# A two-branch attention kernel: operation order from a refitted plan, the middle score tiles in one exponential, value products after all scores

## The chip, the cores and the metric

The kernel runs on one core of a Trainium2 chip. Five engines work side by side, each through its own queue in order: TensorE (PE, matmuls; its weight loads are listed apart as PEld), VectorE (DVE), ScalarE (ACT), GpSimd (POOL) and SyncE (SP), which here only issues transfers. They wait for each other by semaphores. The metric is the device time from the first to the last instruction, in microseconds.

## The reference, cut to what matters

Two attention branches read the same x (2048 tokens, 640 columns, 32 heads of 20), and a gate mixes them.

```python
# branch A: linear attention with softmax feature maps
phi(t) = concat(softmax(t @ w_phi), softmax(-t @ w_phi))
kv, z  = sum_s phi(k) v,  sum_s phi(k)
a      = (phi(q) @ kv) / (phi(q) @ z + 1e-6) @ wo
# branch B: 4 segments of 512 tokens, one after the other
p      = softmax(q k^T * 20**-0.5 + causal mask)          # inside the segment
mem    = (phi(q) @ M) / (phi(q) @ z + 1e-6)               # phi(t) = t+1 if t>0 else exp(t)
o      = sigmoid(beta) * mem + (1 - sigmoid(beta)) * p @ v
M, z   = M + phi(k)^T v, z + sum phi(k)                   # carried to the next segment
b      = o @ wo
out    = g * a + (1 - g) * b,   g = sigmoid(sum(x * gate_w))
```

## The kernel before, in words

**A plan made when the program is built.** The class `Graph` holds a list of operations. Each call of `op` adds one with the engines it may run on, a duration that the plan believes, the tiles it reads and writes, and a priority `pr` (lower goes first). `schedule` then plays the machine forward: for every engine it looks at the ready operations, computes with `est` when each could start (engine free, operands ready, buffers and PSUM banks free), and takes the one with the lowest priority among those that could start within `DELTA` = 0.12 of the earliest. The result is a fixed order for each queue. `emit` writes the instructions in this order with the semaphore waits that the data needs. The believed durations are therefore no part of the program that runs. They only decide the order, and with it which wait stands ahead of which work.

**Priorities.** They are sums of constants: branch B's step g of segment n has 8n + g, its projections, value projection, memory and output work have offsets such as `BN`, `VN`, `MM`, `OT`; branch A's key work starts at `AK` and steps by 1.021 for each of its 16 token tiles, its query work at `AQ` and steps by 4.075 for each of four segments. So the two branches are woven together over the whole span.

**Branch B, one step (`b_step`, L909).** One of 8 head groups (4 heads) of one of 4 segments; 32 steps. Scores are made transposed, key tile by key tile (128 keys each, j = 0 to 3), for 4 heads at once, in three bursts (L923): j = 0 (4 matmuls of 512 columns); j = 1 and 3 together (384 and 128 columns in one bank of each head); j = 2 (256 columns). Each burst fills four PSUM banks. For the first two bursts these are two separately claimed pairs of banks; for the third, one claim of two neighbouring pairs (`joint`, tile size 5 in `tile_avail`). ScalarE turns the scores into exponentials in SBUF (`expT`): two ACTIVATEs of 128x1024 for each of the first two bursts (`expair`, L933), one of 128x1024 over all four banks for the third (`exp2`, L952). GpSimd zeroes what the causal mask hides (L938, four selects of 128x512 in a step). The value products `pv` (L978, 40 matmuls of 21 columns) come in two halves: b = 0 for query tiles 0 and 1, which need key tiles 0 and 1; b = 1 for query tiles 2 and 3, which need all. They wait for the step's last burst in the order (`after=[self.lastqk]`). From segment 1 on, the memory products (L982) go with them. `combine` on VectorE (L1002 to L1027) divides, scales and adds the two into `oB`. Two buffers of `expT` alternate.

**Branch B, the rest.** `b_proj` (L782, L803) projects queries, keys and values of a segment; `b_mem` updates the memory (L858, L872); `b_out` transposes `oB` by a transfer (in the last segment by TensorE, L1046).

**Branch A.** `a_k`, once per token tile: key and value projections (L1065, L1066), two exponentials (L1072), sum, reciprocal and product on VectorE (L1080, L1082, L1083), a transposing transfer of the result (`TT`, issued at L614), and then two adds of the transposed tile into `acc` (L1090, L1092). `a_kv` (L1113, L1124) makes the products with the values, four tiles at a time. `a_q` (L1167 to L1237) does the query side of one segment, `final` (L1268, L1269) both output projections of a token tile into one sum.

The lines that the plan's view of the machine rests on, and the claim for the last wait:

```python
def d_act(n):
    return 0.16 + n * 0.00079
...
    self.dma("sp", ..., transpose=True, dur=1.36, lat=2.5, name="TT")
...
    self.op("pe", ..., pv, ..., claim=[self.oB], after=[self.lastqk], name=f"PV{n},{g}")
```

Of the kernel before, what the change touches and what calls it, by code (L numbers as in the profile page):

```python
# [7 lines left out]
ALU = mybir.AluOpType  # L8
AX = mybir.AxisListType

# [21 lines left out]
def d_act(n):  # L32
    return 0.16 + n * 0.00079


def d_dve(n, mode=1, psum=False):
    return (0.15 if psum else 0.08) + n / (960.0 * mode)
# [6 lines left out]
def d_mm(*ns):  # L44
    return sum(max(n / 2200.0, 0.035) for n in ns)


class Op:
    __slots__ = ("name", "engs", "dur", "fn", "reads", "writes", "claim", "pr", "deps", "users", "tiles", "nleft", "stream",
                 "start", "end", "idx", "dma", "inc", "key", "val", "vc", "lat", "extra", "succ")  # L50


class Tile:
    def __init__(self, name, shape, dtype, pool):
        self.name, self.shape, self.dtype, self.pool = name, shape, dtype, pool
        self.ops = []
        self.h = {}
        self.qk = False
        self.slot = None
        self.prev = ()  # L60
        self.t = None
        self.left = 0

# [38 lines left out]
class Graph:  # L102
# [5 lines left out]

    def op(self, engs, dur, fn, R=(), W=(), pr=0.0, claim=(), name="", dma=False, lat=0.0, after=()):
        o = Op()  # L110
        if isinstance(engs, str):
            engs = (engs,)
        if not isinstance(dur, dict):
            dur = {e: dur for e in engs}
        o.engs, o.dur, o.fn, o.pr, o.name, o.dma, o.lat = engs, dur, fn, pr, name, dma, lat
        o.claim = list(claim)
        deps = list(after)
        tl = []
        for (t, k) in R:
            deps += t.touch(o, k, False)  # L120
            tl.append(t)
        for (t, k) in W:
            deps += t.touch(o, k, True)
            tl.append(t)
        o.reads, o.writes = R, W
        o.tiles = list(dict.fromkeys(tl))
        o.deps = [d for d in dict.fromkeys(deps) if d is not o]
        o.idx = len(self.ops)
        o.stream = None
        o.succ = []  # L130
        o.inc = False
        o.extra = []
        self.ops.append(o)
        return o

    def schedule(self):
# [39 lines left out]
        def tile_avail(t, commit=False):  # L176
# [5 lines left out]
            if isinstance(p, PsumPool):  # L182
                n = t.shape
                if n == 1:
                    best = None
                    for b in range(8):
                        if bank_occ[b] is None:
                            lone = bank_occ[b ^ 1] is None
                            c = (bank_t[b] + (0.3 if lone else 0.0), b)
                            if best is None or c < best:  # L190
                                best = c
                    if best is None:
                        return None
                    if not self.filler_ok(fillers, t):
                        return None
                    if commit:
                        claim_banks(t, [best[1]])
                    return bank_t[best[1]]
# [18 lines left out]
            for s in p.slots:  # L217
                m = 0.0
                ok = True
                for oc in s.occ:  # L220
                    if oc.left > 0:
                        ok = False
                        break
                    for d in oc.ops:
                        m = max(m, d.end)
                if ok and (best is None or m < best[0]):
                    best = (m, s)
# [19 lines left out]

        def est(o, e):
            st = max(free[e], dep_time(o, e))
            qs = [t for t in o.tiles if t.qk and t.slot is None]  # L250
            if qs:
                ps = sorted(max(bank_t[2 * k], bank_t[2 * k + 1]) for k in range(4) if bank_occ[2 * k] is None and bank_occ[2 * k + 1] is None)
                if len(ps) < len(qs):
                    return None
                st = max(st, ps[len(qs) - 1] + LAT)
            for t in o.claim:
                a = tile_avail(t)
                if a is None:
                    return None
                st = max(st, a + LAT)  # L260
# [17 lines left out]
        while done < n:  # L278
# [39 lines left out]
            free[e] = o.end  # L318
            if o.dma:
# [46 lines left out]
    def emit(self):  # L366
# [6 lines left out]
        for q in qs:  # L373
            for i in range(RING):
                allsem[("q", q, i)] = qsem[q][i]
        for o in self.order:
            ds = dict.fromkeys(o.deps)
            for t in o.tiles:
                if any(w[0] is t for w in o.writes):
                    for d in t.prev:  # L380
                        ds[d] = None
            o.extra = [d for d in ds if d is not o]
# [70 lines left out]
class GatedMix(Graph):  # L453
# [174 lines left out]
    def setup(self):  # L628
# [41 lines left out]
        def sel(v, pat, base, cm):  # L670
            op("pool", 0.6, lambda e: e.affine_select(v(), v(), pattern=pat, compare_op=ALU.is_ge, fill=0.0, base=base,
                                                      channel_multiplier=cm), W=[(Mm, "*")], pr=-4)
# [16 lines left out]
        for c in range(NCH):  # L689
# [6 lines left out]
            op("pe", 0.3, tr, R=[(xr, "*"), (idt, "*")], W=[(pt, 0)], pr=-30 + 0.1 * c, name="x0tr")  # L696
# [33 lines left out]
    def fuse(self, wT, Wd, ic, pr):  # L730
# [12 lines left out]
        self.op("pe", 6 * 0.06, mm, R=[(wT, "*"), (BD, "*")], W=[(pt, 0), (pt, 1)], pr=pr, name="fuse")  # L743
# [16 lines left out]
    def b_proj(self, n):  # L760
# [3 lines left out]
        if n == 0:  # L764
            pts = [self.pst("q0", 1) for c in range(NCH)]
            for kc in range(NCH):
# [5 lines left out]
                self.op("pe", 1.3, mm, R=[(self.WB, (0, a, kc)) for a in range(2)] + [(xT, (0, kc))], W=[(p, 0) for p in pts], pr=base - 3 + 0.1 * kc, name="q0proj")  # L772
# [19 lines left out]
        for i in range(4):  # L792
            self.dma("sp", qk[32 * i:32 * i + DH, 5:8, :, :].rearrange("p c w t -> p c (w t)"), scr.rearrange("(m i d) w t -> i d m (w t)", i=4, m=3)[i],
                     R=[(sT, "*")], W=[(qk, f"r{i}")], pr=prr, dur=0.36, lat=2.6, name="relr")
        for tl in range(4):
# [11 lines left out]
            self.op("act", 0.22, lambda e, t=t, pt=pt: e.activation(self.eg[:, t:t + 1], self.pf(pt, 1, 128, 1), ACT.Exp, scale=-1.0),  # L807
# [22 lines left out]
    def b_mem(self, n):  # L830
# [6 lines left out]
        for c in range(NCH):  # L837
            self.dma("sp", lambda c=c: pk[:, :, 128 * c:128 * (c + 1)], qk[:, c, 1, :], R=[(qk, (1, c))],
                     W=[(pk, c)], pr=8 * n + self.KT[0] + self.KT[1] * c, transpose=True, dur=(1.27 if n else 1.7), lat=2.0, name="kT")
        for tl in range(4):  # L840
# [7 lines left out]
            self.op("dve", 0.56, lambda e, tl=tl, tm=tm: e.tensor_tensor(pk[:, tl, :], pk[:, tl, :], tm[:, :], ALU.min),  # L848
# [12 lines left out]
        self.op("pe", 40 * 0.04, mm, R=[(pk, ("t", tl)) for tl in range(4)] + [(vt, tl) for tl in range(4)] + [(vt, "one")], W=[(mp, 0), (mp, 1)], pr=pr, name="Mmm")  # L861
# [14 lines left out]
    def b_pq(self, n):  # L876
        qk = self.qk[n % 2]
        self.pq = {}
        for c in range(NCH):
# [7 lines left out]
            self.op("dve", 0.47, lambda e, pq=pq, tm=tm: e.tensor_tensor(pq[:, :], pq[:, :], tm[:, :], ALU.min),  # L887
# [14 lines left out]
    def b_step(self, n, g):  # L902
# [7 lines left out]
        def burst(js, joint=False):  # L910
            if joint:
                pt = self.pst("QK", 5)
# [14 lines left out]
            self.lastqk = self.op("pe", 0.14 + sum((LSEG - 128 * j) / 2370.0 + 0.03 for j, _ in js), mm, R=rqk, W=pts, claim=[ex], pr=s, name=f"QK{n},{g}")  # L927
# [12 lines left out]
        p0 = burst([(0, 0)])  # L940
        expair(p0, 0, 0)
        mask(0, lambda: ex[:, :, 0:128], [[0, 4], [1, 128]], 512, [(0, 0), (0, 1)])
        p1 = burst([(1, 0), (3, 384)])
        expair(p1, 512, 1)
        mask(1, lambda: ex[:, :, 512:640], [[0, 4], [1, 128]], 512, [(1, 0), (1, 1)])
        mask(3, lambda: ex[:, :, 896:1024], [[0, 4], [1, 128]], 512, [(1, 0), (1, 1)])
        p2 = burst([(2, 0)], True)[0][0]
# [5 lines left out]
        self.op("act", d_act(1024), exp2, W=[(p2, i) for i in range(4)] + [(ex, 2)], pr=s + 0.02, name="exp2")  # L953
# [4 lines left out]
        for b in range(2):  # L958
# [26 lines left out]
            self.op("pe", cnt * 0.0285 + (0.06 * len(parts) if am else 0), pv, R=R, W=[(ad, b if n else 0)], pr=s + self.PVP[0], claim=[self.oB], after=[self.lastqk], name=f"PV{n},{g}")  # L985
# [46 lines left out]
    def b_out(self, n):  # L1032
        oB = self.oB
        for qi in range(4):
# [4 lines left out]
            if n < SEG - 1:  # L1039
                self.dma("sp", lambda oT=oT: oT[:, :, :], lambda qi=qi: oB[:, qi, :], R=rd, W=[(oT, "*")], pr=pr, transpose=True, dur=1.28, lat=2.2, name="oTB")  # L1040
# [7 lines left out]
            self.op("pe", 5 * 0.055, tr, R=rd + [(self.ident, "*")], W=[(pt, 0)], claim=[oT], pr=pr, name="oTBtr")  # L1048
# [3 lines left out]
    def a_k(self, t):  # L1052
# [27 lines left out]
        self.op("dve", 1.42, lambda e: e.tensor_reduce(rz[:, :], Ev(), axis=AX.X, op=ALU.add),  # L1080
                R=[(E, 0), (E, 1)], W=[(rz, "*")], pr=pr, name="Zsum")
        self.op("dve", 0.5, lambda e: e.reciprocal(rz[:, :], rz[:, :]), W=[(rz, "*")], pr=pr, name="Zrec")  # L1082
        self.op("dve", d_dve(1280), lambda e: e.tensor_tensor(  # L1083
            Ev(), Ev(), rz[:, :].rearrange("p (h o) -> p h o", o=1).to_broadcast([128, 2 * H, DH]), ALU.mult),
            R=[(rz, "*")], W=[(E, 0), (E, 1)], pr=pr, name="Anorm")
        self.spread(E, T2, pr)
# [10 lines left out]
    def spread(self, E, T, pr):  # L1097
        self.dma("sp", lambda: T[:, :, :], lambda: E[:, :, :].rearrange("p s n -> p (s n)"), R=[(E, 0), (E, 1)], W=[(T, 0), (T, 1)], pr=pr, transpose=True,
                 dur=1.36, lat=2.5, name="TT")
        return T  # L1100

    def a_kv(self, S):
        pr = self.AK[0] + self.AK[1] * (4 * S + 4)
        ts = [4 * S + i for i in range(4)]
        for s in range(2):
# [10 lines left out]
            self.op("pe", 20 * 0.08, mm, R=[(self.Et[t], s) for t in ts] + [(self.vt[t], "*") for t in ts], W=[(pt, 0), (pt, 1)], pr=pr, name="kv")  # L1116
# [10 lines left out]
    def a_fin(self):  # L1127
        pr = self.AK[0] + self.AK[1] * 16
        zf, K1 = self.zf, self.KVZ1
        self.op("dve", 1.3, lambda e: e.tensor_reduce(zf[:, :, :].rearrange("p s c -> p (s c)"), self.acc[:, :, :], axis=AX.X, op=ALU.add),  # L1130
# [25 lines left out]
    def a_q(self, S):  # L1156
# [34 lines left out]
        op("pe", 1.1, zmm, R=[(ET, s) for ET in ETs for s in range(2)] + [(Mk, c) for c in range(NCH)], W=[(zt, 0)],  # L1191
# [13 lines left out]
        op("pe", 0.25, rtr, R=[(rh, 0), (rh, 1), (self.ident, "*")], W=[(tp, 0)], pr=prz, name="rtr")  # L1205
        self.evac(512, lambda: rT[:, :], lambda: self.psbf[0:64, 1024 * tp.t[0]:1024 * tp.t[0] + 512], W=[(tp, 0), (rT, "*")], pr=prz, name="rT_ev", mode=2)
        for c in range(NCH):
            pt = self.pst("rb", 1)
            op("pe", 0.28, lambda e, c=c, pt=pt: e.matmul(self.pf(pt, 0, 0, LSEG), lhsT=self.Bsel[:, c, :], rhs=rT[:, :], start=True, stop=True),
# [4 lines left out]
        for tl in range(4):  # L1214
# [17 lines left out]
            op("pe", 12 * 0.062, mm, R=kall + [(ET, s) for ET in ETs for s in range(2)], W=[(pt, 0), (pt, 1)], claim=[oA, sm], pr=pru, name="U")  # L1232
# [9 lines left out]
            if S < SEG - 1:  # L1242
                self.dma("sp", lambda oT=oT: oT[:, :, :], lambda oA=oA: oA[:, :], R=[(oA, 0), (oA, 1)], W=[(oT, "*")], pr=pru + 0.5,
                         transpose=True, dur=1.28, lat=2.2, name="oTA")
            else:
# [6 lines left out]
                op("pe", 5 * 0.055, tr, R=[(oA, 0), (oA, 1), (self.ident, "*")], W=[(pt, 0)], claim=[oT], pr=pru + 0.5, name="oTAtr")  # L1252
# [102 lines left out]
```

## Time and profile before

| | before |
|---|---|
| median of 3 runs, us | 345.99 (343.73 to 347.31) |
| profiled span, us | 345.6 |
| mean granted TensorE clock | 0.965 |
| exponentials of branch B, 128x1024 (L933) | 128, 123.2 us |
| the same over four banks (L952) | 32, 32.8 us |
| masks on GpSimd (L938) | 128, 88.4 us |
| value products (L978) | 1280, 42.9 us |
| TT transfers, issue to landing | median 3.7 us |

How to read the profile: TensorE's matmuls overlap, and their ends are modelled, so a mean duration (387 ns for 512 columns) is more than the distance between two starts (213 to 218 ns in the timeline). For TensorE what counts is its idle time, and whether the granted clock is 1.00 or 0.50 in a stretch. Idle time of the other engines costs nothing in itself; a wait of VectorE or ScalarE matters when TensorE later waits for what stood behind it in the same queue.

### The profile page before, as it was taken

To read this page: it belongs to the slowest core of one execution; us is meant where nothing else is said; L and a number is where in the kernel's file an instruction comes from. 1 tells how busy PE (TensorE), PEld (TensorE's weight loads), DVE (VectorE), ACT (ScalarE), POOL (GpSimd) and SP (SyncE) were. 2 spreads that over 40 slices of the span, in tenths; PEclk is the share of its full clock that TensorE was granted. 3 is DMA by queue.
4 is the path that set the end of the run, shared out by engine and by line. 5 is a ranking of instruction groups with operands and counts; after the bars stand their busy time and mean duration, and the time that the engine had idled before them with its cause. 6 is when DMAs were issued, how large, how long until landed. Compare 5 with 4: busy or idle time off the path is not lost.

```text
span 345.6 us, 8962 instructions
## 1 busy us (share of the span) xinstructions
PE 309.6 (90%) x3824; PEld 180.0 (52%) x3824; DVE 243.0 (70%) x480; ACT 262.5 (76%) x361; POOL 107.0 (31%) x170
## 2 busy tenths in 40 slices
PE   3998979988999998979986999999998899898896
PEld 2454444545555545655534555565555554655763
DVE  4705856999889999969897769852667466546760
ACT  3459966998899888578996599649996569867531
POOL 7842231343313433223232123112232213222300
PEclk9999987999999999699999899999999999999699
DMA  7999692364426426662237003752023440221001
GB/s 202 263 243 185 107 119 38 55 112 44 100 39 113 43 40 91 116 102 41 40 98 189 2 3 41 110 100 59 21 16 59 90 69 3 48 68 41 2 21 57
DMA packets 68824, 27.52 MB, mean 80 GB/s; under 512 B 60401, under 2 KB 66865, under 8 KB 68785
## 3 DMA queue, kind: packets, MB, share of 16 engines
q1 hardware_dynamic: 68688, 26.92, 41.7%
q8 instruction: 30, 0.49, 0.6%
q0 software_dynamic: 96, 0.04, 0.3%
q14 instruction: 10, 0.07, 0.1%
HBM read 7.57 MB, written 4.59 MB: 35 GB/s over the span
## 4 chain that ended last, share of the span: by engine, by line
PE 53%; DVE 19%; ACT 17%; DMA 9%; issue 1%; POOL 1%
PE ps L1268 9%; ACT expT L933 8%; DMA TT<-E 8%; PE ps L782 6%; PE ps L1065 6%; PE ps L978 6%; PE ps L1167 4%; PE ps L923 3%; PE ps L803 3%; PE ps L1228 3%; DVE acc L1092 2%; DVE E L1083 2%; PE ps L1269 2%; ACT expT L952 2%; PE ps L769 2%; DVE cb L1024 2%
## 5 line engine op out<-in xcount | busy, mean ns | idle before, releaser
L938 POOL TENSOR_SCALAR_AFFINE_SELECT expT<-expT 128x512 bf16<-128x512 bf16 x128 | 88.4, 692 | 214.7 <-ACT expT L933 156.4
L933 ACT ACTIVATE expT<-ps 128x1024 bf16<-128x1024 f32 x128 | 123.2, 1027 | 7.8 <-PE ps L923 7.2
L978 PE MATMUL ps<-v1B,expT 128*128 128x21 bf16 x1280 | 42.9, 173 | 5.8 <-DVE vA L753 1.8
L978 PEld LDWEIGHTS ps<-v1B,expT 128*128 128x128 bf16 x1280 | 38.9, 96 | 15.1 <-POOL expT L938 4.3
L782 PE MATMUL ps<-xT,WB 128*128 128x512 bf16 x175 | 43.9, 387 | 2.8 <-DVE oB L1019 2.3
L923 PE MATMUL ps<-qk 20*128 20x128 bf16 (+3 forms) x512 | 35.1, 307 | 7.4 <-ACT expT L933 1.5
L952 ACT ACTIVATE expT<-ps 128x1024 bf16<-128x1024 f32 x32 | 32.8, 1025 | 7.3 <-PE ps L923 6.8
L752 ACT ACTIVATE out<-ps 128x640 bf16<-128x640 f32 x16 | 11.2, 703 | 28.4 <-PE ps L1269 28.4
L923 PEld LDWEIGHTS ps<-qk 20*128 20x128 bf16 x512 | 10.5, 92 | 32.4 <-issue 7.7
L1167 PE MATMUL ps<-xT,WqA 128*128 128x512 bf16 x100 | 26.1, 400 | 0.4 <-ACT ET L1172 0.2
L782 PEld LDWEIGHTS ps<-xT,WB 128*128 128x128 bf16 x175 | 15.3, 98 | 21.3 <-DVE oB L1019 2.6
L1065 PE MATMUL ps<-WvA,xT 128*128 128x512 bf16 x80 | 26.1, 412 | 0.1
L1172 ACT ACTIVATE ET<-ps 128x512 bf16<-128x512 f32 x40 | 23.5, 608 | 3.6 <-PE ps L1167 3.1
L1268 PE MATMUL ps<-Wo,oTA 128*128 128x512 bf16 x80 | 23.5, 380 | 1.8 <-ACT expT L933 1.2
L1083 DVE TENSOR_TENSOR E<-E,z 128x1280 bf16<-128x1280 bf16 x16 | 24.5, 1534 | 0.4
L1072 ACT ACTIVATE E<-ps 128x640 bf16<-128x640 f32 x32 | 22.8, 712 | 2.6 <-PE ps L1066 2.2
L1065 PE MATMUL ps<-WkA,xT 128*128 128x512 bf16 x80 | 23.5, 381 | 1.0 <-DVE KVZacc L1124 0.6
L803 PE MATMUL ps<-WvB,xT 128*128 128x512 bf16 x80 | 23.8, 381 | 0.4 <-DVE cb L1024 0.4
L1080 DVE TENSOR_REDUCE z<-E 128x64 f32<-128x1280 bf16 x16 | 23.6, 1478 | 0.8 <-ACT E L1072 0.8
L1268 PE MATMUL ps<-Wo,oTB 128*128 128x512 bf16 x80 | 23.5, 380 | 0.0
L1002 DVE TENSOR_TENSOR cs<-ps,epsv 128x32 f32<-128x32 f32 x24 | 4.5, 187 | 25.2 <-PE ps L982 25.2
L1092 DVE TENSOR_TENSOR acc<-acc,TT 128x640 bf16<-128x640 bf16 x31 | 17.0, 548 | 5.5 <-DMA TT<-E 5.0
(129 smaller groups left out, 583.4 us busy)
## 6 DMA issues: line engine op xcount, KB each, us to landing
out_dram<-out SPq DMA_DIRECT2D x16, 160.0 KB, 2.0
scr<-qk SPq DMA_DIRECT2D x16, 120.0 KB
qk<-scr SPq DMA_DIRECT2D x16, 120.0 KB
stq<-in_B_wq_dram SPq DMA_DIRECT2D x5, 160.0 KB
WvB<-in_B_wv_dram SPq DMA_DIRECT2D x1, 800.0 KB, 9.3
WvA<-in_A_wqkv_dram SPq DMA_DIRECT2D x1, 800.0 KB, 5.3
Wo<-in_A_wo_dram SPq DMA_DIRECT2D x1, 800.0 KB
Wo<-in_B_wo_dram SPq DMA_DIRECT2D x1, 800.0 KB
```

Source lines behind the costliest of these rows:

```text
L782: r = e.matmul(self.pf(pt, 0, 0, LSEG), lhsT=self.WB[:, w, kc, 128 * c:128 * (c + 1)], rhs=xT[:, kc, LSEG * n:LSEG * (n + 1)], start=(kc = ...
L803: e.matmul(self.pf(pt, 0, 0, 512), lhsT=l, rhs=self.WvB[:, kc, 0:512], start=(kc == 0), stop=(kc == 4))
L923: r = e.matmul(self.pf(pts[i][0], pts[i][1], c0, N), lhsT=qk[32 * i:32 * i + DH, g, 1, 128 * j:128 * (j + 1)], rhs=qk[32 * i:32 * i + DH, ...
L933: self.op("act", d_act(1024), lambda e, p=p, pt=pt: e.activation(ex[:, 2 * p:2 * p + 2, off:off + 512], self.pbanks(pt, 0, 2, 512), ACT.Ex ...
L938: self.op("pool", d_pool(n_el), lambda e: e.affine_select(view(), view(), pattern=pat, compare_op=ALU.is_ge, fill=0.0, base=0, channel_mul ...
L952: return e.activation(ex[:, :, 1024:1280].rearrange("p (k b) c -> p k b c", k=2), src, ACT.Exp, scale=scale)
L978: r = e.matmul(self.pf(ad, b, 84 * q2 + 21 * i, 21) if n else self.pf(ad, 0, 84 * qi + 21 * i, 21), lhsT=ex[:, i, c0:c0 + 128], rhs=vt[:, ...
L1065: e.matmul(self.pf(pt, 0, 0, 512), lhsT=l, rhs=W[:, kc, 0:512], start=(kc == 0), stop=(kc == 4))
L1083: self.op("dve", d_dve(1280), lambda e: e.tensor_tensor(Ev(), Ev(), rz[:, :].rearrange("p (h o) -> p h o", o=1).to_broadcast([128, 2 * H, ...
L1092: self.op("dve", 0.5, lambda e, h=h: e.tensor_tensor(acc[:, :, :], acc[:, :, :], T2[:, :, 64 * h:64 * h + 64], ALU.add), R=[(T2, 0), (T2, ...
L1167: r = e.matmul(self.pf(pt, 0, 0, LSEG), lhsT=self.WqA[:, kc, 128 * c:128 * (c + 1)], rhs=xT[:, kc, LSEG * S:LSEG * (S + 1)], start=(kc == ...
L1268: e.matmul(self.pf(pt, 0, 0, 512), lhsT=l, rhs=self.Wo[:, c, 0:512], start=(c == 0), stop=(c == 9))
```

## The change

It does four things.

1. The durations and latencies that the plan believes are fitted again, and two more effects are told to it: 0.094 for going over to a burst of scores from other matmuls (`tiled`), and the claim of the first five query projections, which need five free banks together (`group`). The transfer latencies become longer, for TT 3.6 (6.0 for the first and the last tile) instead of 2.5.
2. `NUDGE` adds a number to the priority of some 290 operations, found by a local search over the plan.
3. The scores of key tiles 1 and 3 go into one claim of two neighbouring pairs of banks and are read by one ACTIVATE of 128x2048 (`exp4`) instead of two of 128x1024.
4. Both halves of the value products wait for the step's last exponential (`self.lastmask`, which holds `exp2`), beside the last burst.

In `emit`, GpSimd's operations next to a select that builds the memory mask (`Mmsel`) also wait for the one before. The rest (a cached end time of a buffer's last use, `oc.done`) speeds the planning up.

The diff, cut to its core:

```diff
+NUDGE = {6: 1.6, 7: 1.65, 8: -2.2, 9: -0.45, 11: -1.7, 33: -4.85, 34: -2.7, 60: -2.95, 70: -0.25, 97: -4.3, 99: -4.6, 103: -0.35, 105: 0.4, 107: -0.4,
...
 def d_act(n):
-    return 0.16 + n * 0.00079
+    return 0.167 + n * 0.00075
...
-    return (0.15 if psum else 0.08) + n / (960.0 * mode)
+    return 0.12 + n / (1024.0 * mode) if psum else 0.08 + n / (960.0 * mode)
...
-    return sum(max(n / 2200.0, 0.035) for n in ns)
+    return sum(max(n / 2360.0, 0.0355) for n in ns)
...
-        o.engs, o.dur, o.fn, o.pr, o.name, o.dma, o.lat = engs, dur, fn, pr, name, dma, lat
+        o.engs, o.dur, o.fn, o.pr, o.name, o.dma, o.lat = engs, dur, fn, pr + NUDGE.get(len(self.ops), 0.0), name, dma, lat
...
-            st = max(free[e], dep_time(o, e))
+            st = max(free[e] + (0.094 if o.tiled and not self.tiled else 0.0), dep_time(o, e))
...
+            if any(t.group > bank_occ.count(None) for t in o.tiles if t.slot is None):
+                return None
...
+            if o.stream == "pool":
+                if lp is not None and "Mmsel" in (o.name, lp.name):
+                    ds[lp] = None
+                lp = o
...
+            for p in pts:
+                p.group = NCH
...
-        def burst(js, joint=False):
+        def burst(js, joint=0):
             if joint:
-                pt = self.pst("QK", 5)
+                pt = self.pst("QK", joint)
...
-        p0 = burst([(0, 0)])
-        expair(p0, 0, 0)
+        def exp4(pt, off, j):
+            def f(e):
+                a, b = pt.t[0] // 2, pt.t[2] // 2
+                src = self.ps[:, :].rearrange("p (k b c) -> p k b c", k=4, b=2)[:, a:b + 1:b - a, :, :]
+                return e.activation(ex[:, :, off:off + 512].rearrange("p (k b) c -> p k b c", k=2), src, ACT.Exp, scale=scale)
+            self.op("act", d_act(2048), f, W=[(pt, i) for i in range(4)] + [(ex, (j, 0)), (ex, (j, 1))], pr=s, name="exp")
+        expair(burst([(0, 0)]), 0, 0)
...
-        p1 = burst([(1, 0), (3, 384)])
-        expair(p1, 512, 1)
+        exp4(burst([(1, 0), (3, 384)], 5)[0][0], 512, 1)
...
-        self.op("act", d_act(1024), exp2, W=[(p2, i) for i in range(4)] + [(ex, 2)], pr=s + 0.02, name="exp2")
+        self.lastmask = self.op("act", d_act(1024), exp2, W=[(p2, i) for i in range(4)] + [(ex, 2)], pr=s + 0.02, name="exp2")
...
-            self.op("pe", cnt * 0.0285 + (0.06 * len(parts) if am else 0), pv, ..., after=[self.lastqk], name=f"PV{n},{g}")
+            self.op("pe", cnt * 0.026 + (0.04 + 0.037 * len(parts) if am else 0), pv, ..., after=[self.lastqk, self.lastmask], name=f"PV{n},{g}")
...
-                 dur=1.36, lat=2.5, name="TT")
+                 dur=1.36, lat=(3.6 if 0 < t < 15 else 6.0), name="TT")
```

## The prediction

> **What bounds the kernel now.** I began with the page's busy table and its forty slices.
>
> ```profile
> PE 309.6 (90%) x3824; PEld 180.0 (52%) x3824; DVE 243.0 (70%) x480; ACT 262.5 (76%) x361; POOL 107.0 (31%) x170
> ...
> PE   3998979988999998979986999999998899898896
> ...
> PEclk9999987999999999699999899999999999999699
> ```
>
> TensorE is busy 309.6 of 345.6 us; nothing else is over 76%. So a gain has to come out of TensorE's 36.0 idle microseconds or out of stretches in which its clock is down (the sixes, sevens and eights of PEclk). The next view was busy time by stretch, asked for over those dips:
>
> ```profile
> core 0: us, PE busy (x) PEld busy (x) DVE busy (x) ACT busy (x) POOL busy (x), PEclk, DMA share, GB/s
> ...
> 48.70:55.50 6.80, 5.58 (x20) 2.16 (x21) 6.14 (x12) 2.37 (x4) 1.49 (x3) 0.50 0.26 19
> 137.40:144.20 6.80, 6.69 (x87) 4.64 (x84) 6.50 (x13) 4.06 (x5) 2.12 (x4) 0.50 0.76 135
> 192.00:195.40 3.40, 3.40 (x12) 1.19 (x9) 3.30 (x8) 1.97 (x3) 0.63 (x1) 0.50 0.00 0
> 321.70:328.50 6.80, 5.60 (x90) 5.38 (x91) 5.13 (x13) 2.73 (x4) 2.09 (x3) 0.50 0.01 2
> ```
>
> In four stretches the granted clock is 0.50: 21.3 us of TensorE work that would take about 10.6 us at full clock. Two of them follow a pause. I read these in the chain of work, cut to 40-56 us and 176-193 us:
>
> ```profile
> 42.54 5.91 DMA TT<-E
> ...
> 48.48 0.48 DVE acc L1090
> ...
> 49.37 0.50 DVE oB L1019
> 49.87 0.05 issue
> 49.92 2.31 PE ps L782 x5
> ```
>
> ```profile
> 180.22 7.29 DMA TT<-E
> 187.51 0.02 issue
> 187.53 0.50 DVE acc L1092
> ...
> 189.30 0.83 DVE cb L1024
> ```
>
> VectorE works its queue in order. The add of a transposed tile (L1090, L1092) was placed when the plan thought the tile landed; the tile was late, and the combines behind it (L1019, L1024), which free PSUM for TensorE, waited too. In the waits by engine TensorE shows both, each in one long piece:
>
> ```profile
> PE ps L694 <- DMA xr<-in_A_x_dram: 5.8, 1, 5.8
> PE ps L1113 <- DVE cb L1024: 3.5, 2, 2.9
> PE ps L782 <- DVE oB L1019: 2.3, 1, 2.3
> PE ps L978 <- DVE vA L753: 1.8, 1, 1.8
> ```
>
> The first line is the load of x at the start, which no order removes; another 3 us at the end (last output copy at 342.70) are fixed too. What an order can win at most is 36.0 - 5.8 - 3 = 27 us of idle time and 10.6 us of slow clock: a ceiling near 38 us, a floor near 308.
>
> [...] 1024 columns take 1.023 us [...] and pairs end 1.84 to 1.94 us after their start. [...] The stretches here have lengths of 6.8 and 3.4 us[...]. [...] the score bursts (20 rows) alternate with full matmuls, and the weight loads ahead of L923 idle for 7.7 us in 27 short pieces with no releaser[...].
>
> **The change part by part.**
>
> *One exponential for the middle tiles.* Per step (32 steps) two 128x1024 ACTIVATEs over key tiles 1 and 3 become one of 128x2048. [...] ScalarE has 83 us of idle time, and TensorE waits for it in short pieces only, so I count 1 us on the path. The masks for tiles 1 and 3 (L938) cover all four heads and already wait for both halves, so nothing moves there. The cost is in PSUM: the first pair of banks comes free about 0.93 us later, and the burst now needs two neighbouring free pairs where any two did before. That is 32 x 2 banks x 0.93 = 60 bank-microseconds of 8 x 320 = 2560, 2%. Between 0 and 0.2 us of added wait per step: 0 to 6 us; I take 2.
>
> *Value products wait for all scores.* The first half of the products (L978) could start when tiles 0 and 1 were masked; now it waits for the last exponential (L952, 1.02 us) as well. At 75.62 us in the trace the burst for tile 2 runs, at 75.84 the first half starts, and the exponential comes only at 76.11: that first half (0.36 to 0.47 us) filled a gap and must be replaced. Queued behind it on TensorE is whatever is next in the order, and the combine on VectorE waits for it. If nothing replaces it: 32 x 0.4 = 13 us. If a projection group stands there (1.08 to 1.36 us apiece by the timeline, and some 140 of them exist) it is 0; the planner now knows of the wait and puts them there. I take 1 us. [...]
>
> *Refitted durations and latencies.* No instruction changes. What matters is that the TT transpose is planned with 1.36 + 6.0 us for the first and last tile (3.6 latency otherwise) where it was 1.36 + 2.5 = 3.9. Measured were 5.9 us at 42.5 and 7.3 at 180.2 (behind the two Wo loads). So both blockages of VectorE should go. By stretch:
> - 47.6 to 55.5: pause 2.3, slow clock 5.58 / 2 = 2.8; 5.1 us.
> - 180 to 195.4: pauses 1.8 and 2.9, slow clock 3.40 / 2 = 1.7; 6.4 us.
> - 137.4 to 144.2: slow clock 6.69 / 2 = 3.3 us, after several short pauses with small matmuls.
> - 146.7 to 149.0: two waits for exponentials, 1.47 + 0.43 = 1.9 us.
>
> Sum 16.7 us. The last dip (321.7 to 328.5) lies in the closing dependent chain of combine, transpose and final product and I leave it as it is.
>
> *Nudged priorities.* Some 290 operations move in the order. This is what can turn the better costs into fewer pauses: the 27 us of idle time holds, beside the 8.9 us of pauses counted above, 18 us in waits mostly under 1 us. An order can shorten them or make new ones; I take no net from it beyond the stretches, and give the range for it: 10 us either way.
>
> *Edits at nothing.* The grouped claim of five banks for the first query projection is what happens already at 8 to 15 us; the added waits between mask-building selects (22 of 0.56 us on GpSimd) lie before 20 us, and GpSimd then sits idle for 6.8 us until the first score mask, so up to 22 x 0.1 is hidden.
>
> Sum: -16.7 - 1 - 1 + 2 + 1 = -15.7, of which I keep nine tenths, because transfers will land late elsewhere: -14. 346 - 14 = 332 us.
>
> **The rivals.**
>
> *Deep gain.* The order also takes half of the 18 us of short waits and the last clock dip: 332 - 9 - 3 = 320. For it: idle time is spread over the whole span, and filler exists everywhere. Against: VectorE and ScalarE run at 0.85 to 0.97 of the stretches between 60 and 180 us (19.4 and 19.2 of 20 at 60-80), so in this half there is little slack to move.
>
> *The gain turns into other waits.* VectorE's 243 us and ScalarE's 262 stay, and the middle stretches are bound by three engines at once. The two blockages go, but other tiles land late or bank claims block: half of 14 is lost or more; 340 to 345.
>
> *Slower.* The wait on the last exponential and the claim of two neighbouring pairs stall TensorE in most steps: +13 (products not replaced) +6 (banks) -5 (one blockage gone) = +14, lessened by what fill there is to about 352. For it: score bursts already wait for exponentials to free banks (weight loads at L923: 5.0 and 3.2 us in 20 pieces). [...]
>
> **How the numbers follow.** Forecast (326 to 340): 0.50. Deep gain (below 326): 0.22. Gain turned into waits (340 to 349.5): 0.14, of which 0.06 lies below 342.5. Slower (above 349.5): 0.14. Faster by over 1% is 0.50 + 0.22 + 0.06 = 0.78; within 1% 0.08; slower 0.14. The range 319 to 349 leaves out about 0.06 below and 0.14 above.
>
> **What would show it right or wrong.** Right: no wait of VectorE for TT above 1 us; no clock dip near 50 and 190 us; TensorE idle near 24 us instead of 36; ACTIVATEs of 128x2048 near 1.88 us; ScalarE's busy time down by 3 us. Wrong: a large new line of TensorE waiting at L978 for the exponential of L952's successor, L923's weight loads waiting longer for ScalarE, or a first stretch of 20 us that is later than before. A fall of TensorE's busy time without fewer pauses would mean that the clock alone moved it.

## The result, and the profile after

The changed kernel takes 335.54 us (median of 4 runs, 333.77 to 336.42) against 346.11 us before: a ratio of 0.970, 95% interval 0.963 to 0.977, or 10.6 us. The forecast was 332 us in a range of 319 to 349. Here and below, ratios and intervals leave out runs over 1.5% above the fastest of the same kernel, so they can differ a little from the quotient of the medians.

The page of the changed kernel: the busy table, and TensorE's busy share and granted clock in forty slices.

```profile
PE 301.9 (90%) x3776; PEld 179.2 (54%) x3824; DVE 246.7 (74%) x483; ACT 259.4 (78%) x326; POOL 106.4 (32%) x170
...
PE   2989999899999888989989999898899987997996
...
PEclk9999999999999998999999999999999778999699
```

In this trace 48 of 3824 matmul records are missing, so its TensorE figure is low. A second profile of the same kernel has them all: 305.5 us busy in a span of 331.6, so 26.1 us idle instead of 36.0; about 24 had been forecast. The dips of the clock (the stretches at half clock) near 50 and 190 us are gone; three new ones stand close together from 261 us on. By the clock records half-clock stretches fill 23.9 us in the kernel before, 20.5 in this profile and 17.1 in the second one, so most of the gain is idle time.

VectorE's waits for the TT transfer, before and then after (us in total, times, longest), and the merged exponential on the page of the changed kernel (busy us, mean ns):

```profile
DVE acc L1092 <- DMA TT<-E: 5.0, 6, 2.3
...
DVE acc L1090 <- DMA TT<-E: 2.9, 1, 2.9
```

```profile
DVE acc L1135 <- DMA TT<-E: 0.5, 1, 0.5
```

```profile
L983 ACT ACTIVATE expT<-ps 128x2048 bf16<-128x2048 f32 x32 | 60.1, 1878 | 5.0 <-PE ps L962 4.9
```

To see where the time came from I lined the two traces up by work instead of by time. Every weight load counts with the distance of two starts of its matmul in a dense stretch (in the trace of the kernel before 216 ns for 512 columns, 56 for 128, 26 for 21, and so on; 288.3 us in all for either kernel). The table says when each kernel had done so much; the score bursts, whose four matmuls overlap (four of 512 columns took 0.39 us in all at 45.70 us of the kernel before), can be weighted in more than one way, which moves a lead by up to some 1 us, most in the last rows.

| work done, us | before at | after at | lead of after |
|---|---|---|---|
| 35 | 46.5 | 45.8 | 0.7 |
| 45 | 61.3 | 55.6 | 5.7 |
| 115 | 141.3 | 133.3 | 8.0 |
| 125 | 155.9 | 145.4 | 10.6 |
| 145 | 176.9 | 165.7 | 11.2 |
| 155 | 192.1 | 176.6 | 15.5 |
| 165 | 203.9 | 187.1 | 16.8 |
| 225 | 269.6 | 252.2 | 17.4 |
| 245 | 290.9 | 280.6 | 10.3 |
| 285 | 338.9 | 327.8 | 11.1 |

The lead grows in two leaps, 5.0 us between 46 and 61 us of the kernel before and 5.6 us between 177 and 204: the two places in which VectorE's queue had stood behind a TT transfer. A third, of 2.6 us, lies at 141 to 156, where before the clock was halved until 144 us. Then 7.1 us are lost again in the last segment (work 225 to 245, after 252 us); in the second profile it is about 4.5.

### The profile page after: what moved, and what is told of

Its sections match the earlier page's. It is cut to its first block, busy times and chain, and to the rows that moved or that the text cites. A ratio compares the mean times of both kernels' runs of the same rounds, so it can differ in the third digit from the quotient of the medians.

```text
span 334.5 us, 8874 instructions
## 1 busy us (share of the span) xinstructions
PE 301.9 (90%) x3776; PEld 179.2 (54%) x3824; DVE 246.7 (74%) x483; ACT 259.4 (78%) x326; POOL 106.4 (32%) x170
## 4 chain that ended last, share of the span: by engine, by line
PE 64%; DVE 19%; ACT 10%; DMA 4%; issue 2%; SPq 0%; DVEq 0%
PE ps L1311 10%; PE ps L821 8%; PE ps L1021 7%; PE ps L1108 6%; PE ps L1210 6%; PE ps L962 5%; PE ps L842 4%; PE ps L1271 4%; ACT expT L972 3%; PE ps L1312 3%; ACT expT L983 3%; DVE E L1126 2%; PE ps L808 2%; DVE z L1123 2%; DMA TT<-E 2%
## 5 line engine op out<-in xcount | busy, mean ns | idle before, releaser
L972 ACT ACTIVATE expT<-ps 128x1024 bf16<-128x1024 f32 x64 | 61.7, 1025 | 7.2 <-PE ps L962 7.2
L983 ACT ACTIVATE expT<-ps 128x2048 bf16<-128x2048 f32 x32 | 60.1, 1878 | 5.0 <-PE ps L962 4.9
L1021 PE MATMUL ps<-v1B,expT 128*128 128x21 bf16 x1280 | 41.8, 173 | 2.0 <-DVE M L909 0.9
L821 PE MATMUL ps<-xT,WB 128*128 128x512 bf16 x164 | 40.2, 379 | 0.9 <-issue 0.3
L962 PE MATMUL ps<-qk 20*128 20x512 bf16 (+3 forms) x512 | 35.4, 309 | 6.0 <-ACT expT L983 1.7
L995 ACT ACTIVATE expT<-ps 128x1024 bf16<-128x1024 f32 x32 | 32.7, 1022 | 2.7 <-PE ps L962 2.3
L962 PEld LDWEIGHTS ps<-qk 20*128 20x128 bf16 x512 | 10.4, 92 | 29.6 <-issue 10.3
L1210 PE MATMUL ps<-xT,WqA 128*128 128x512 bf16 x93 | 24.5, 396 | 1.2 <-issue 0.8
L1108 PE MATMUL ps<-WvA,xT 128*128 128x512 bf16 x75 | 23.3, 393 | 1.3 <-DVE cb L1067 0.9
L1126 DVE TENSOR_TENSOR E<-E,z 128x1280 bf16<-128x1280 bf16 x16 | 23.9, 1493 | 0.4
L1108 PE MATMUL ps<-WkA,xT 128*128 128x512 bf16 x74 | 22.4, 387 | 0.5 <-ACT E L1115 0.5
L842 PE MATMUL ps<-WvB,xT 128*128 128x512 bf16 x72 | 21.7, 381 | 0.6 <-ACT v1B L789 0.5
L789 ACT ACTIVATE qk<-ps 128x512 bf16<-128x512 f32 x26 | 15.5, 599 | 8.0 <-PE ps L821 4.4
```

The lines of the kernel that those rows point to most:

```text
L821: r = e.matmul(self.pf(pt, 0, 0, LSEG), lhsT=self.WB[:, w, kc, 128 * c:128 * (c + 1)], rhs=xT[:, kc, LSEG * n:LSEG * (n + 1)], start=(kc = ...
L842: e.matmul(self.pf(pt, 0, 0, 512), lhsT=l, rhs=self.WvB[:, kc, 0:512], start=(kc == 0), stop=(kc == 4))
L962: r = e.matmul(self.pf(pts[i][0], pts[i][1], c0, N), lhsT=qk[32 * i:32 * i + DH, g, 1, 128 * j:128 * (j + 1)], rhs=qk[32 * i:32 * i + DH, ...
L972: self.op("act", d_act(1024), lambda e, p=p, pt=pt: e.activation(ex[:, 2 * p:2 * p + 2, off:off + 512], self.pbanks(pt, 0, 2, 512), ACT.Ex ...
L983: return e.activation(ex[:, :, off:off + 512].rearrange("p (k b) c -> p k b c", k=2), src, ACT.Exp, scale=scale)
L995: return e.activation(ex[:, :, 1024:1280].rearrange("p (k b) c -> p k b c", k=2), src, ACT.Exp, scale=scale)
```

## The experiments

The theory: the order made the gain, mostly by no longer having VectorE wait for late transfers ahead of work that frees PSUM; the merged exponential and the added wait are worth about nothing. The first rival: the structure made it. The second: the refitted latency alone did. The third: the order is better everywhere by a little, and the two places don't matter. The median of the kernel before differed between the groups of runs (346.1 to 348.8 us), so ratios to the runs beside are compared; runs of one group carry the same median.

**The changed kernel again** (group A, median of before 347.3), unchanged.

> The changed kernel itself, as the yardstick of the three runs beside it. Every theory expects about 335.5 us, a ratio of 0.970 to the kernel before.

Measured: 335.91 us, ratio 0.969 (0.964 to 0.974).

**The exponential split, same order** (group A).

```diff
-                return e.activation(ex[:, :, off:off + 512].rearrange("p (k b) c -> p k b c", k=2), src, ACT.Exp, scale=scale)
+                for p in range(2):
+                    r = e.activation(ex[:, 2 * p:2 * p + 2, off:off + 512], self.pbanks(pt, 2 * p, 2, 512), ACT.Exp, scale=scale)
+                return r
```

> The changed kernel with every 128x2048 exponential issued as two of 128x1024 at the same place of the same order, banks freed together as in the changed kernel. Theory (the order made the gain): [...] the span by 0 to 2 us, so 335.5 to 337.5. Rival (the merged read made the gain): half or more of the 10.6 us is lost, 341 or more.

Measured: 337.07 us, ratio 0.972 (0.966 to 0.977). ScalarE is busy 261.1 us instead of 259.2: 1.9 us or 0.06 us per step, less than the 3 us forecast. In time it is some 0.9 us by the ratios, within the intervals. The merged read isn't what made the gain.

**The products without the added wait, same order** (group A).

```diff
-            o.extra = [d for d in ds if d is not o]
+            o.extra = [d for d in ds if d is not o and ((o, d) not in self.soft or any(d in t.prev for t in o.tiles))]
...
+            if b == 0:
+                self.soft.add((pvop, self.lastmask))
```

> The changed kernel, same order, in which the first half of the value products no longer waits for the last exponential (except in 8 of 32 steps where it needs that wait for its PSUM bank). Theory: the order already puts other work there, so the wait costs nothing: within 1 us of the changed kernel. Rival (the added wait takes back part of the gain): 2 us or more faster than the changed kernel. The second rival (the wait helps because products come together) can't show here, since the order stays.

Measured: 337.13 us, ratio 0.970 (0.964 to 0.975): no difference from 0.969 that can be told. In this order the added wait of the first half costs nothing; that of the second half was not taken out.

**Three dense matmuls more in each step of the last segment** (group A).

```diff
+                if n == 3 and b == 0:
+                    for _ in range(3):
+                        e.matmul(self.pf(ad, b, 0, 512), lhsT=self.xT[:, 0, 0:128], rhs=self.xT[:, 0, 0:512], start=True, stop=True, skip_group_check=True)
```

> The changed kernel with three more matmuls of 128x512 ahead of the first half of the value products in each of the last segment's 8 steps (their sums are overwritten, so the output is the same). They add 24 x 0.216 = 5.2 us of TensorE work. Theory (the four half-clock stretches from 260 us on come because the 3.4 us before hold little but matmuls of 7 to 21 columns and score bursts, though TensorE reads as busy): the stretches at 260, 271 and 281 us go, worth 3 x 3.4 / 2 = 5.1 us, and the span stays within 2 us, the granted clock above 0.98. Rival (the dips come from idle pauses or at fixed times): the dips stay and the kernel is 3 to 5 us slower.

Measured: 339.82 us, ratio 0.978 (0.973 to 0.983), so 0.009 x 347 = 3.2 us slower than the changed kernel beside it (3.9 by the medians): the rival's time. The granted clock was 0.985 instead of 0.974. Of the stretches that the changed kernel's profile in this group had at 268 and 278 us, the second is gone and the first is there still. A stretch at 131 us, far from the added work, is missing too, so the added work need not be what removed the second one; such dips come and go from run to run (see the last section). The stretch that stayed, with the 3.4 us before it (columns as in the prediction):

```profile
263.70:267.10 3.40, 2.58 (x17) 0.57 (x16) 2.52 (x5) 3.35 (x5) 0.65 (x2) 1.00 0.01 1
267.10:270.50 3.40, 3.40 (x52) 2.04 (x53) 1.10 (x3) 0.91 (x3) 1.25 (x2) 0.50 0.00 0
```

TensorE was busy for 2.58 of 3.40 us in the window before, without one matmul of 7 to 21 columns, so these are not needed for a dip. But 13 of its 17 matmuls use only 20 or 64 of the array's 128 rows, among them:

```profile
264.15 0.60 PE L1255 MATMUL ps<-rT,Bsel 64*128 64x512 bf16 x2
264.69 0.40 PE L962 MATMUL ps<-qk 20*128 20x384 bf16 x8
265.32 0.39 PE L1255 MATMUL ps<-rT,Bsel 64*128 64x512 bf16 x1 [0.24 <-DVE ET L1257]
```

The last section takes this up.

**The order of before, four adds moved** (group B, median of before 347.85). The adds of the first TT tile go behind the next two combines, those of the tile of 180 us behind the combine and two sums.

```diff
+        move([dv[ch[0]], dv[ch[1]]], dv[second])
+        move([dv[ch[28]], dv[ch[29]]], dv[ch[30] - 1])
```

> The kernel before with its order kept, except that VectorE's adds of the first TT tile stand behind the two combines that followed them (near 48 us), and those of the tile transferred at 180 us behind the combine and the first two key-value sums. Theory (a late transfer at the head of VectorE's queue blocked TensorE at these two places and cost 5.1 and 6.4 us with the slow clock after it): 7 to 11 us faster than before, 335 to 339, and no half clock near 49 and 192 us. Rival (the two places are not on the path, the gain came from the order as a whole): less than 3 us, 343 to 346.

Measured: 341.39 us, ratio 0.977 (0.971 to 0.983): 2.3% or 7.9 us (6.5 by the medians) for four moved VectorE instructions, at the lower edge of what the theory gave. The pause of 2.93 us before L1113 is 0.18 us now, and no half clock stands near 192 us, though one does at 178.9. At the first place the pause only moved, and a half clock follows it at 56.0. TensorE and VectorE in the timeline of this run:

```profile
49.15 0.39 PE L923 MATMUL ps<-qk 20*128 20x512 bf16 x4
49.39 0.46 DVE L1090 COPY acc<-TT 128x640 bf16<-128x640 bf16 x1 [2.12 <-DMA TT<-E]
...
54.38 0.68 DVE L753 CAST qk<-ps 128x512 bf16<-128x512 f32 x1
...
55.21 0.29 PE L923 MATMUL ps<-qk 20*128 20x256 bf16 x4 [3.12 <-DVE qk L753]
```

The add still waits 2.12 us for the tile; the cast that now stands behind it is late, and TensorE pauses 3.12 us for that cast.

**The same, the first pair behind the next cast** (group C, median of before 348.77).

```diff
-        move([dv[ch[0]], dv[ch[1]]], dv[second])
+        cast = [i for i, o in enumerate(dv) if o.name == "qk_ev" and i > second][0]
+        move([dv[ch[0]], dv[ch[1]]], dv[cast])
```

> As the run with the two pairs of adds moved, but the first pair stands still further back, behind the cast of the next query-key projection (7 VectorE instructions later, past the landing at 49.4 us). In the first version VectorE still waited 2.1 us for the transfer and TensorE paused 3.1 us for that cast, with a half clock at 56 us. Theory: that pause and dip go, 3.1 + 1.7 us more than the first version, so some 9 to 13 us faster than before, ratio 0.963 to 0.974. Rival (pauses only move on to the next tile): like the first version, 0.975 to 0.980.

Measured: 338.96 us, ratio 0.972 (0.968 to 0.977), 9.7 us. Lined up by work, it gains 4.6 us at the first place (45.2 and 55.4 us for work 35 and 45) and 4.1 us at the second (169.9 and 192.8 us for 145 and 165), against 5.0 and 5.6 in the changed kernel. Busy time from 45 to 60 us, first in the kernel before and then in this run:

```profile
45.00:60.00 15.00, 12.67 (x145) 6.16 (x142) 8.97 (x18) 10.09 (x14) 3.29 (x5) 0.77 0.53 70
```

```profile
45.00:60.00 15.00, 14.28 (x178) 7.60 (x177) 13.93 (x23) 14.70 (x20) 6.68 (x8) 1.00 0.51 74
```

TensorE did 178 matmuls instead of 145 at a clock of 1.00 instead of 0.77. With TensorE's, ScalarE's and SyncE's orders as they were, and no new number in the plan, most of the change's gain is there. The converse, the changed kernel with its adds put back ahead of the combines, was not run.

**Only the TT latency in the plan of before** (group B).

```diff
-                 dur=1.36, lat=2.5, name="TT")
+                 dur=1.36, lat=(3.6 if 0 < t < 15 else 6.0), name="TT")
```

> The kernel before, planned anew with the longer TT latency (3.6, and 6.0 for the first and last tile) and nothing else. Theory: the two blockages go, but the whole order changes and priorities chosen for the old plan no longer fit, so the gain is partly or wholly lost: 338 to 352, with no wait of VectorE for TT above 1 us. Rival (the latency alone made the gain): 335 to 338.

Measured: 354.53 us, ratio 1.018 (1.011 to 1.024). Slower, beyond even the range that I gave, and I was wrong about the waits as well. VectorE's waits in this run, and then its adds at the second place in the kernel before and in this run:

```profile
DVE acc L1092 <- DMA TT<-E: 8.5, 3, 4.3
DVE acc L1090 <- DMA TT<-E: 1.6, 1, 1.6
```

```profile
187.53 1.02 DVE L1092 TENSOR_TENSOR acc<-acc,TT 128x640 bf16<-128x640 bf16 x2 [2.34 <-DMA TT<-E]
```

```profile
188.34 1.02 DVE L1092 TENSOR_TENSOR acc<-acc,TT 128x640 bf16<-128x640 bf16 x2 [4.27 <-DMA TT<-E]
```

The first place still costs VectorE 1.6 us, the second more than before, and two further tiles (near 56 and 140 us) are waited for as well. The rival (the latency alone) falls.

**Only the structure, on the plan of before** (group B): `exp4` and the added wait, put in with the old durations.

> The kernel before, planned anew with the 128x2048 exponential (four neighbouring banks) and the products' wait, old durations and no nudges. Theory (the structure is worth little by itself, and an order not searched for it loses): 345 to 354. Rival (the structure made the gain): 336 to 341.

Measured: 359.91 us, ratio 1.030 (1.021 to 1.038). Slower still than I thought. TensorE waits for the merged exponential, but the new order also makes VectorE wait for TT for 16.8 us, where it was 7.9:

```profile
PE ps L923 <- ACT expT L947: 6.1, 9, 0.9
```

```profile
DVE acc L1097 <- DMA TT<-E: 11.6, 7, 3.1
DVE acc L1095 <- DMA TT<-E: 5.2, 1, 5.2
```

So this run doesn't show what the structure costs by itself: the order changed with it, as in the run with the TT latency only, which was slower without any of the structure.

**The changed kernel without nudges** (group B): `NUDGE = {}`.

> The changed kernel with all nudges zero: refitted durations, merged exponential, wait. Theory (the nudges made most of the gain): 341 to 348. Rival (the refit alone does it): 335 to 338.

Measured: 346.86 us, ratio 1.001 (0.998 to 1.004). On top of the refit and the structure the nudges are worth the whole 3.1%. VectorE's wait for TT is 0.4 us here too, and at work 165 the kernel leads by 9.5 us, but by the end only 1.7 are left: what was won at the two places was lost again after it.

**Without nudges, old structure** (group C).

```diff
-        exp4(burst([(1, 0), (3, 384)], 5)[0][0], 512, 1)
+        p1 = burst([(1, 0), (3, 384)])
+        expair(p1, 512, 1)
...
-after=[self.lastqk, self.lastmask]
+after=[self.lastqk]
```

> Refitted durations and latencies, all nudges zero, and the old structure: two 128x1024 exponentials over two separate pairs of banks, products that do not wait for the last exponential. Beside it stands the same plan with the new structure, 346.9 us. Theory (the structure is worth about nothing by itself): 343 to 350. Rival (the structure made the gain): 351 or more. Second rival (the structure costs, and the nudges repaired it): 342 or less.

Measured: 349.85 us, ratio 1.003 (1.001 to 1.006), against 1.001 with the new structure: nothing between them that can be told apart.

**Without nudges, the TT latency back at 2.5** (group C).

> The changed kernel with all nudges zero and the TT latency of the plan set back to 2.5. Theory (knowing the latency is what the refit brings): VectorE waits for TT by 3 us or more in all, 3 to 8 us slower than without nudges, 350 to 355. Rival (the refit works through its other numbers): 345 to 349.

Measured: 361.26 us (355.40 to 361.51), above the 350 to 355 expected, with no interval; even the lowest is 355.40 / 348.77 = 1.019. VectorE waits for TT 5.8 us in all, against 0.4 with the longer latency. That speaks for the latency within the refit, but other parts of the order changed with it.

**Every other nudge** (group C).

```diff
+NUDGE = {k: v for i, (k, v) in enumerate(NUDGE.items()) if i % 2}
```

> The changed kernel with every other nudge set to zero. Theory (the nudges are one found order, not a sum of small improvements): most of their gain is lost, 341 to 352. Rival (each nudge brings its share): half of the 11 us between no nudges and all, 340 to 342.

Measured: 356.97 us, ratio 1.020 (1.014 to 1.026). Half of the nudges are 2% worse than none, slower than I had allowed for. They act as one order, found together, and not as a sum of improvements. (`NUDGE` holds 247 numbers, not some 290.)

## Why the prediction was right

*The two blockages of VectorE.* Predicted 5.1 and 6.4 us; the lead grows by 5.0 and 5.6 there, and moving four adds in the old order gives 4.6 and 4.1. That these waits cost the time is shown. One part of the step was wrong: that the longer latency in the plan would be enough. For the second place the reason given doesn't hold: the tile sent at 180.2 us is the fifteenth of 16, not the last, so the new plan believes 1.36 + 3.6 = 4.96 us for it, not 7.36, where the chain before showed 7.29. With the latency alone VectorE's waits for TT were 10.1 us and the kernel 1.8% slower; with the whole refit but no nudges they are gone (0.4 us), but the time does not fall. What helped in the old order was the place of the adds. Which numbers of the new plan put them in a good place was not tried.

*The stretch 137 to 149 us.* Predicted 5.2 us; the lead grows by 2.6. This term was too large: the changed kernel still has a half-clock stretch near there, of 3.4 us at 131.2, where the kernel before has 6.8 us.

*The merged exponential.* Predicted 1.88 us each, measured 1.878; predicted 3 us of ScalarE time, measured 1.9 by splitting it again. The 3 us were an estimate that the trace of before did not show: there a pair of 128x1024 takes 1.94 us (at 55.54 us, for one), 0.06 more than the merged one, or 1.9 us in 32 steps. ScalarE's busy time fell by the 3.1 us forecast (262.5 to 259.4), but partly by luck: the exponentials concerned account for 1.4 of it (123.2 us before, 61.7 + 60.1 after), and copies that the new order gives to VectorE for most of the rest.

*The added wait and the banks.* Predicted 1 - 1 + 2 = 2 us lost; the 1 us that comes off was my estimate for the two halves coming together, and no trace showed it. The wait of the first half alone measures 0 in the order found, and with the refit and no nudges the structure makes no difference that can be told (1.001 with it, 1.003 without). Put into the plan of before it came out 3.0% slower; TensorE then waits 6.1 us for the merged exponential, which the slower rival had feared, but VectorE's waits for TT grew too. What the banks cost was not measured alone.

*Nudges: "no net beyond the stretches, 10 us either way".* The lead reached 17.4 us, more than the 14 forecast, of which the three stretches make 5.0 + 5.6 + 2.6 = 13.2 (16.7 were summed); the other 4 us came in small pieces. Then 7.1 us of it went again in the last segment, which I had not looked at. The chain of waits of the changed kernel shows how:

```profile
256.76 3.78 ACT expT L972 x4
260.59 1.19 PE ps L1271 x12
```

Two steps' first exponentials stand in a row on ScalarE, TensorE has only small matmuls and pauses meanwhile, and its clock halves, at 260.9 us by the clock records. The windows of 3.4 us around this time:

```profile
257.10:260.50 3.40, 2.70 (x85) 2.04 (x81) 2.49 (x7) 3.40 (x5) 0.63 (x1) 1.00 0.64 122
260.50:263.90 3.40, 3.09 (x20) 1.66 (x21) 2.89 (x7) 1.80 (x2) 1.90 (x3) 0.56 0.15 50
```

The clock halves three times, at 261, 271 and 281 us, an estimated 3 x 3.4 / 2 = 5.1 us of the 7.1. In the kernel before, the clock is 1.00 from 200 to 320 us. But the new order is not the whole reason: with the old order of TensorE and the adds moved further, a half-clock stretch stands at 258.0 us too. What the new order itself costs in the last segment is not shown.

*The clock.* This is the term that was most out of size. The forecast took 2.8 + 1.7 + 3.3 = 7.8 us from 17.1 us of half clock that would go. That much went at the three places, but new stretches came, and the total fell by 3.4 us only (6.8 in the second profile), worth an estimated 1.7 to 3.4 us at a clock of 0.50. Idle time fell by 9.9 us where about 12 had been forecast. That 332 lies so near to 335.5 is therefore partly luck: small gains that nobody had forecast stood against a loss that nobody had forecast.

## What to carry to other kernels

Where one queue is fixed in advance, look for the instruction that waits for a transfer at its head, and at what stands behind it: four adds moved behind that work gave 2.8%, which can't be told apart from the whole new plan's 3.0%. A searched order is one piece: take a part of its numbers, or change one latency in the plan, and the result is as good as a new draw, here between 1.00 and 1.04 of the time before. And follow a gain to the end of the span, for what one stretch wins another may give back.

## What the hardware showed that I had not expected

By the clock records of the kernel before, half-clock stretches begin at 48.7, 137.4, 192.0, 321.7 and 345.6 us. They lie 88.75, 54.61, 129.71 and 23.89 us apart, which is 26, 16, 38 and 7 times 3.413 us to within 0.01 us, and last 6.83, 6.83, 3.41 and 6.83 us (the end of the record cuts the last one short). In the changed kernel they begin at 131.2, 260.9, 271.2, 281.4 and 308.7 us, again whole multiples of 3.413 us apart, and last 3.41 us four times and 6.83 us once. Their place against the kernel's work differs from run to run: in two profiles of the changed kernel the same work gave dips at 261, 271 and 281 us in one, and at 268 and 278 us in the other (mean clock from 250 to 290 us 0.87 and 0.91).

In the last 3.41 us of full clock ahead of a half clock, TensorE of the kernel before was busy, by its modelled ends, for a share of 0.47 to 0.85 (the very end apart). The pause of 47.6 to 49.9 us was only about half over when the clock halved at 48.7. Busy time does not decide, as two stretches of the kernel before show. A half clock follows the first and none the second:

```profile
318.31:321.72 3.41, 2.90 (x51) 1.36 (x49) 2.98 (x7) 2.75 (x3) 1.27 (x2) 1.00 0.11 41
```

```profile
178.36:181.77 3.41, 1.63 (x12) 0.54 (x11) 3.41 (x4) 3.38 (x6) 2.59 (x3) 1.00 0.77 235
```

Work weighted by rows tells these two apart. It is an estimate of mine from the start times and shapes in the trace: each matmul counts as its columns x 0.42 ns (512 columns follow each other in 215 ns) x its rows / 128, spread over its columns' time, which is twice as long at half clock (there 512 columns follow each other in 427 ns). The first of the two stretches then holds 0.29 of its 3.41 us, the second 0.38. With the whole trace of the kernel before cut into 98 such stretches, the eight that a half clock follows hold 0.09 to 0.37 and the 90 others 0.38 to 0.99. The two groups come within 0.005 of each other, in one trace, so no threshold is shown by it. By this count score matmuls of 20 rows, and products of 21 columns that start 25 ns apart but count 9, fill TensorE's busy time with little work. The count was made afterwards; no run tested it, and what the hardware itself counts is not shown.
